# The third batch's loads moved to the software DMA queue, behind the output weights

## The chip, the core and the metric

One core of a Trainium2 chip runs the whole kernel. The metric is device time in microseconds (us) per execution: the median of three runs. The matmul engine is PE (TensorE), the vector engine DVE (VectorE), the activation engine ACT (ScalarE), the general engine POOL (GpSimd), and SP (SyncE) only issues transfers. A core has 16 DMA engines. Transfers issued by SP go on queue q1 (its descriptors are made in hardware), those issued by POOL on queue q0 (made in software on POOL); only POOL's transfers change the type on the way, from float32 in DRAM to bf16 on chip.

## The reference

Inputs q, k and v are float32 of shape (8 batches, 8 heads, 576 rows, 64). Attention with pooled keys and values feeds a gated layer:

```
k_p, v_p = mean of k, v over groups of 8 rows        # 72 rows
attn     = softmax(q @ k_p.T / 8);  x = attn @ v_p   # x: 4608 x 512
h        = x @ w_in                                  # 512 x 2048
out      = (h * cos(h)) @ w_out                      # 2048 x 512
```

## The kernel before

The schedule is written out by hand: each engine runs its instructions in the order of the program. Attention for batch b gives 576 rows of `xT`. The gated layer works in nine tiles (`t` = 0 to 8) of 512 rows: `up` (lines 252 to 263) multiplies by the input weights into three pairs of PSUM banks, ACT takes the cosine into a tile `cos`, DVE multiplies into `g_sb`, and `down_mm` (line 265) multiplies by the output weights. The attention of batch `t + 1` is woven into the `down` matmuls of tile t (lines 333 to 369).

Before the loop stands a start (lines 283 to 324). POOL issues, in this order: k of batch 0 (`k_b`, four transfers), q of batch 0 (`q_main`, `q_rem`, four), v of batch 0 (two), the input weights (four), k, q and v of batch 1 (two each), the output weights (four). SP issues k and v of batch 2 (lines 300 and 301) at the same time, as float32, into the two `kv_st` buffers: a main piece of 64 partitions and a rest of 8 each, 1.18 MB per tensor. Then PE pools k of batch 0 with matmuls (line 142), transposes q (line 168), makes scores, sums and values (lines 199, 208, 222); the values' first step pools v (line 150). The first `up` follows.

From batch 2 on, k and v are pooled on POOL (`pool_kv`, lines 114 to 120, three additions each) out of `kv_st`. At the end of tile t's step the program emits `pool_kv` for batch t + 2. `load_kv` of the batch after waits on SP until `kv_st` is free again; q goes on POOL's queue (`load_q`, line 90) in tile t's step, for batch t + 2. In the step of tile 1, PE transposes the pooled k of batch 2 (line 190), and later uses its v.

A tile that is asked for again waits until its oldest buffer of the same name is free: `kv_st` has two buffers, `q_main` and `q_rem` two each, `cos` three. POOL's transfers count on eight semaphores in turn, so a ninth transfer waits until the first has landed.

Of the kernel before, what the change touches and what calls it, by code (L numbers as in the profile page):

```python
# [9 lines left out]
FP32 = mybir.dt.float32  # L10
# [5 lines left out]
TILE = 512  # L16
# [3 lines left out]
def kernel(  # L20
# [9 lines left out]
    nc = tc.nc  # L30
    B, H, S, D = q.shape
# [16 lines left out]
    wpool = ctx.enter_context(tc.tile_pool(name="wpool", bufs=1))  # L48
    kvb = ctx.enter_context(tc.tile_pool(name="kvb", bufs=4))
    kvst = ctx.enter_context(tc.tile_pool(name="kvst", bufs=2))  # L50
    qst = ctx.enter_context(tc.tile_pool(name="qst", bufs=2))
    asb = ctx.enter_context(tc.tile_pool(name="asb", bufs=2))
    msb = ctx.enter_context(tc.tile_pool(name="msb", bufs=3))
    psum = ctx.enter_context(tc.tile_pool(name="psum", bufs=1, space=bass.MemoryType.PSUM))
# [12 lines left out]
    def by_rows(dst, src):  # L67

        for lo, hi in ((0, 64), (64, Sp)):
            yield dst[lo:hi], src[:, lo:hi]  # L70

    def kv_view(src, b):
        return src[b].rearrange("h (p t) d -> h p (t d)", t=POOL)

    def load_kv(b, which, src):
        st = kvst.tile([Sp, H, POOL, D], FP32, name="kv_st", tag="kv_st")
        for o, i in by_rows(st.rearrange("p h t d -> p h (t d)"), kv_view(src, b)):
            nc.sync.dma_start(out=o, in_=i.rearrange("h p n -> p h n"))
        staged[which, b] = st

    def load_kv_cast(b, which, src, halves=1):
# [8 lines left out]
    def load_q(b, halves=1):  # L90
        qm = qst.tile([128, H, 4, D], BF16, name="q_main", tag="q_main")
        qr = qst.tile([64, H, D], BF16, name="q_rem", tag="q_rem")
        hs = H // halves
        for j in range(halves):
            hh = slice(j * hs, (j + 1) * hs)
            nc.gpsimd.dma_start(out=qm[:, hh].rearrange("p h t d -> p h (t d)"),
                                in_=q[b, hh, 0:512, :].rearrange("h (p t) d -> p h (t d)", t=4))
            nc.gpsimd.dma_start(out=qr[:, hh], in_=q[b, hh, 512:S, :].rearrange("h s d -> s h d"))
        pooled["q", b] = (qm, qr)
# [6 lines left out]
    def load_w_out(cg):  # L106
        nc.gpsimd.dma_start(
            out=w_out_sb[cg],
            in_=moe_w_out[cg * 512:(cg + 1) * 512, :].rearrange("(f p) m -> p f m", p=128))
# [23 lines left out]
    def pool_k_mm(b, bank, pjs):  # L133

        kb = staged["k", b]
        if ("kpT", b) not in att:
            att["kpT", b] = asb.tile([128, KCH, Sp], BF16, name="kpT", tag="kpT")
        ps = bank[:, 0:KCH * Sp].rearrange("p (j n) -> p j n", j=KCH)
        for pj in pjs:
            for t in range(POOL):  # L140
                for hp in range(2):
                    nc.tensor.matmul(ps[hp * 64:hp * 64 + 64, pj, :], lhsT=kb[:, 2 * pj + hp, t, :],  # L142
                                     rhs=identity[:Sp, :Sp], start=(t == 0), stop=(t == POOL - 1))
        sl = slice(pjs[0], pjs[-1] + 1)
        nc.vector.tensor_copy(out=att["kpT", b][:, sl, :], in_=ps[:, sl, :])

    def pool_v_mm(b, bank):
        vb = staged["v", b]
        for t in range(POOL):
            nc.tensor.matmul(bank[:Sp, :], lhsT=identity[:Sp, :Sp], rhs=vb[:, :, t, :],  # L150
                             start=(t == 0), stop=(t == POOL - 1))
        dst = asb.tile([Sp, H, D], BF16, name="vp", tag="vp")
        nc.vector.tensor_copy(out=dst, in_=bank[:Sp, :].rearrange("p (h d) -> p h d", h=H))
        pooled["v", b] = dst

    def q_transpose(b, bank, pjs=range(KCH)):

        if ("qT", b) not in att:
            att["qT", b] = asb.tile([128, KCH, S], BF16, name="qT", tag="qT")
        qT = att["qT", b]  # L160
        qb, _ = pooled["q", b]
        n = len(pjs)
        ps = bank.rearrange("p a n -> p (a n)").bitcast(BF16)[:, 0:n * 512].rearrange(
            "p (j t n) -> p j t n", t=4, j=n)
        for i, pj in enumerate(pjs):
            for t in range(4):
                for hp in range(2):
                    nc.tensor.matmul(ps[hp * 64:hp * 64 + 64, i, t, :], qb[:, 2 * pj + hp, t, :],  # L168
                                     identity, is_transpose=True)
        c0 = col_of(b, 0)  # L170
        nc.vector.tensor_copy(out=qT[:, pjs[0]:pjs[-1] + 1, c0:c0 + 512],  # L171
                              in_=ps.rearrange("p j t n -> p j (t n)"))

    def q_transpose_rem(b, bank, pjs=range(KCH)):
        qT = att["qT", b]
        _, qrb = pooled["q", b]
        n = len(pjs)
        ps = bank.bitcast(BF16)[:, 0:n * 64].rearrange("p (j n) -> p j n", j=n)
        for i, pj in enumerate(pjs):
            nc.tensor.matmul(ps[:, i, :], heads(qrb, pj).rearrange("p h d -> p (h d)"),  # L180
                             identity[:64, :64], is_transpose=True)
        c0 = col_of(b, 4)
        nc.vector.tensor_copy(out=qT[:, pjs[0]:pjs[-1] + 1, c0:c0 + 64], in_=ps)  # L183
# [61 lines left out]
    def exp_tables():  # L245
        nc.scalar.preload_act_table_set("natural_log_exp_and_others")  # L246
# [5 lines left out]
    def up(t, fp):  # L252

        h = banks[fp % 3]
        for j in range(2):
            fc = 2 * fp + j
            for ki in range(KCH):
                nc.tensor.matmul(h[:, j, :], lhsT=w_in_sb[fc // 4][:, ki, (fc % 4) * 128:(fc % 4 + 1) * 128],  # L258
                                 rhs=xT[:, ki, t * TILE:(t + 1) * TILE],
                                 start=(ki == 0), stop=(ki == KCH - 1))  # L260
        cos = msb.tile([128, 2, TILE], FP32, name="cos", tag="cos")
        nc.scalar.activation(out=cos, in_=h, func=ACTF.Sin, bias=half_pi[:, :1])  # L262
        nc.vector.tensor_mul(out=g_sb[:, 2 * fp:2 * fp + 2, :], in0=h, in1=cos)  # L263

    def down_mm(o, ms, fc):
        nc.tensor.matmul(o, lhsT=g_sb[:, fc, ms * 128:(ms + 1) * 128],  # L266
                         rhs=w_out_sb[fc // 4][:, fc % 4, :], start=(fc == 0), stop=(fc == FFCH - 1))
# [29 lines left out]
    load_kv_cast(1, "v", v)  # L297
    for cg in range(4):
        load_w_out(cg)
    load_kv(2, "k", k)  # L300
    load_kv(2, "v", v)
    exp_tables()
    LAG = 4
    for j in range(2):
# [21 lines left out]
    for t in range(NT):  # L326
        b = t + 1
        for fp in range(FFCH // 2):
            up(t, fp)
            if t == 0 and fp == 5:  # L330
                pool_k_mm(1, obanks[0], range(KCH))
        more = b < B
        fill = []
        if t == 0:
            outs = [obanks[0], obanks[1], banks[2][:, 0, :], banks[2][:, 1, :]]
            mms = [(ms, fc) for cg in range(4) for ms in range(4) for fc in range(4 * cg, 4 * cg + 4)]
            exp_tables()
            q_transpose(1, banks[0])
            q_transpose_rem(1, banks[1][:, 0, :])
            pool_v_mm(1, banks[1][:, 1, :])  # L340
            main = att_main(1, [banks[0]], banks[1])
            fill = [(i * 7 // 2, f) for i, f in enumerate(main)]
        else:
            outs = [obanks[ms % 2] for ms in range(4)]
            mms = [(ms, fc) for ms in range(4) for fc in range(FFCH)]
            if more:
                early = [lambda: k_transpose(b, banks[2][:, 0, :]),
                         lambda: q_transpose(b, banks[0]),
                         lambda: q_transpose_rem(b, banks[2][:, 1, :])]
                main = att_main(b, [banks[1], banks[0]], banks[2])  # L350
                fill = [(4 + 4 * i, f) for i, f in enumerate(early)]
                fill += [(16 + (i * 5) // 2, f) for i, f in enumerate(main)]
                exp_tables()
        if more and t > 0 and b + 1 < B:
            load_kv(b + 1, "k", k)
            load_kv(b + 1, "v", v)
        if more and b + 1 < B:
            load_q(b + 1)
        fi = 0
        for n, (ms, fc) in enumerate(mms):  # L360
            while fi < len(fill) and fill[fi][0] <= n:
                fill[fi][1]()
                fi += 1
            down_mm(outs[ms], ms, fc)
            if fc == FFCH - 1:
                down_out(t, ms, outs[ms])
        while fi < len(fill):
            fill[fi][1]()
            fi += 1
        if more:  # L370
            sin_tables()
            if b + 1 < B:
                pool_kv(b + 1, "k", nc.gpsimd)
                pool_kv(b + 1, "v", nc.gpsimd)
# [30 lines left out]
```

## Time and profile before

| what | us |
|---|---|
| median of 3 runs | 374.42 (374.41 to 374.74) |
| profiled execution, its own time | 373.32 |
| span of that execution, first to last instruction | 371.6 |
| PE busy | 332.1 (89% of the span) |
| ACT, DVE, POOL busy | 191.8, 156.4, 124.2 |

Times within the profile count from the first instruction. Clock columns give the share of full speed that was granted to PE: 1.00 is 2.4 GHz, 0.50 is 1.2 GHz. GB/s counts the bytes written, so a transfer that turns float32 into bf16 counts two bytes per element.

### The profile page before, as it was taken

To read this page: it belongs to the slowest core of one execution; us is meant where nothing else is said; L and a number is where in the kernel's file an instruction comes from. 1 tells how busy PE (TensorE), PEld (TensorE's weight loads), DVE (VectorE), ACT (ScalarE), POOL (GpSimd) and SP (SyncE) were. 2 spreads that over 40 slices of the span, in tenths; PEclk is the share of its full clock that TensorE was granted. 3 is DMA by queue.
4 is the path that set the end of the run, shared out by engine and by line. 5 is a ranking of instruction groups with operands and counts; after the bars stand their busy time and mean duration, and the time that the engine had idled before them with its cause. 6 is when DMAs were issued, how large, how long until landed. Compare 5 with 4: busy or idle time off the path is not lost.

```text
span 371.6 us, 4965 instructions
## 1 busy us (share of the span) xinstructions
PE 332.1 (89%) x1992; PEld 137.7 (37%) x1992; DVE 156.4 (42%) x201; ACT 191.8 (52%) x280; POOL 124.2 (33%) x80
## 2 busy tenths in 40 slices
PE   0158697998999899989998999899989998999995
PEld 0133244333442344334423442344334433444442
DVE  0021356114662366236632663275337533742641
ACT  1017464364657565756575657565756575611610
POOL 6143299200099009800980098019600000000000
PEclk9999999699999999999999999999999999999999
DMA  7999999502942694169426941693020001002002
GB/s 144 192 149 198 153 188 129 65 1 86 192 92 59 98 201 77 59 111 185 89 53 114 188 91 41 118 196 85 30 58 0 30 28 58 0 28 86 0 30 83
DMA packets 31990, 35.18 MB, mean 95 GB/s; under 512 B 5856, under 2 KB 20448, under 8 KB 31968
## 3 DMA queue, kind: packets, MB, share of 16 engines
q1 hardware_dynamic: 12448, 23.60, 27.6%
q0 software_dynamic: 19520, 11.28, 26.3%
q8 instruction: 15, 0.25, 0.3%
q14 instruction: 7, 0.06, 0.1%
HBM read 36.70 MB, written 9.44 MB: 124 GB/s over the span
## 4 chain that ended last, share of the span: by engine, by line
PE 86%; DMA 5%; DVE 3%; ACT 3%; POOL 1%; issue 1%; DVEq 0%; POOLq 0%
PE bank L258 34%; PE obank L266 34%; DMA q_main<-in_q_dram 5%; PE bank L199 4%; PE bank L208 4%; PE bank L222 3%; PE bank L168 2%; PE bank L150 2%; PE bank L266 2%; DVE xT L227 2%; ACT inv L214 1%; ACT lnc L212 1%; POOL k_b L87 1%; DVE o_sb L271 1%; DVE qT L171 0%
## 5 line engine op out<-in xcount | busy, mean ns | idle before, releaser
L266 PE MATMUL obank<-w_out_sb,g_sb 128*128 128x512 bf16 x544 | 141.4, 383 | 0.0
L258 PE MATMUL bank<-xT,w_in_sb 128*128 128x512 bf16 x576 | 127.6, 382 | 0.0
L262 ACT ACTIVATE cos<-bank,half_pi 128x1024 f32<-128x1024 f32 x72 | 80.2, 1115 | 75.7 <-PE bank L258 75.7
L263 DVE TENSOR_TENSOR g_sb<-bank,cos 128x1024 bf16<-128x1024 f32 x72 | 88.2, 1225 | 54.0 <-ACT cos L262 54.0
L117 POOL TENSOR_TENSOR kv_st<-kv_st 72x2048 f32<-72x2048 f32 x12 | 54.2, 4519 | 110.5 <-DMA kv_st<-in_k_dram 110.5
L258 PEld LDWEIGHTS <-w_in_sb 128*128 128x128 bf16 x576 | 56.6, 99 | 68.9 <-issue 2.4
L266 PEld LDWEIGHTS <-g_sb 128*128 128x128 bf16 x576 | 45.9, 98 | 60.0 <-issue 15.0
L202 ACT ACTIVATE ex<-bank 72x576 bf16<-72x576 f32 x64 | 41.0, 641 | 49.9 <-PE bank L199 48.5
L227 DVE TENSOR_TENSOR xT<-bank,inv 128x288 bf16<-128x288 f32 x64 | 29.3, 458 | 88.9 <-ACT inv L214 84.7
L212 ACT ACTIVATE lnc<-bank 128x288 f32<-128x288 f32 x56 | 23.0, 411 | 32.2 <-PE bank L222 32.2
L271 DVE COPY o_sb<-obank 128x512 f32<-128x512 f32 x34 | 23.4, 687 | 29.4 <-PE obank L266 29.4
L214 ACT ACTIVATE inv<-lnc 128x288 f32<-128x288 f32 x64 | 28.3, 443 | 2.0
L118 POOL TENSOR_TENSOR kv_st<-kv_st 72x1024 f32<-72x1024 f32 x12 | 28.2, 2349 | 0.9
L208 PE MATMUL bank<-ex,ones 72*64 72x288 bf16 x112 | 17.5, 307 | 6.3 <-DVE xT L227 6.3
L222 PE MATMUL bank<-ex,vp 72*64 72x288 bf16 x128 | 20.1, 303 | 3.1 <-DVE xT L227 3.1
L199 PE MATMUL bank<-qT,kpT 64*72 64x288 bf16 x128 | 21.5, 331 | 0.4 <-DVE qT L183 0.4
L142 PE MATMUL obank<-identity,k_b 72*64 72x72 bf16 x128 | 3.6, 227 | 19.2 <-DMA k_b<-in_k_dram 19.2
L208 PEld LDWEIGHTS <-ones 72*64 72x64 bf16 x128 | 8.5, 109 | 32.7 <-issue 32.7
L199 PEld LDWEIGHTS <-kpT 64*72 64x72 bf16 x128 | 7.4, 110 | 26.9 <-issue 26.9
L168 PE MATMUL bank<-identity,q_main 128*64 128x128 bf16 x256 | 9.7, 232 | 2.9 <-DMA q_main<-in_q_dram 2.1
L171 DVE COPY qT<-bank 128x2048 bf16<-128x2048 bf16 (+1 forms) x9 | 9.9, 1105 | 5.1 <-PE bank L168 5.1
L246 ACT ACT_TABLE_LOAD x8 | 10.3, 1283 | 0.9 <-PEq L389 0.7
(34 smaller groups left out, 113.3 us busy)
## 6 DMA issues: line engine op xcount, KB each, us to landing
out_dram<-o_sb SPq DMA_DIRECT2D x32, 256.0 KB, 2.3
kv_st<-in_k_dram SPq DMA_DIRECT2D x6, 1024.0 KB, 8.2
kv_st<-in_v_dram SPq DMA_DIRECT2D x6, 1024.0 KB
q_main<-in_q_dram POOLq DMA_DIRECT2D x7, 512.0 KB, 6.0
w_in_sb<-in_moe_w_in_dram POOLq DMA_DIRECT2D x4, 512.0 KB, 13.2
w_out_sb<-in_moe_w_out_dram POOLq DMA_DIRECT2D x4, 512.0 KB, 15.5
v_b<-in_v_dram POOLq DMA_DIRECT2D x2, 512.0 KB, 16.5
out_dram<-o_sb SPq DMA_DIRECT2D x8, 128.0 KB, 2.3
```

What stands on the lines that cost most here:

```text
L117: eng.tensor_tensor(out=s[:, :, 0:4, :], in0=s[:, :, 0:4, :], in1=s[:, :, 4:8, :], op=ADD)
L118: eng.tensor_tensor(out=s[:, :, 0:2, :], in0=s[:, :, 0:2, :], in1=s[:, :, 2:4, :], op=ADD)
L199: nc.tensor.matmul(pair[:Sp, hp, :SEG], lhsT=kpT[hp * 64:hp * 64 + 64, pj, :], rhs=qT[hp * 64:hp * 64 + 64, pj, sg * SEG:(sg + 1) * SEG])
L202: nc.scalar.activation(out=ex, in_=pair[:Sp, :, :SEG], func=ACTF.Exp, scale=scale / POOL)
L208: nc.tensor.matmul(cs[hp * 64:hp * 64 + 64, :SEG], lhsT=ones[:Sp, :], rhs=ex[:, hp, :])
L214: nc.scalar.activation(out=inv, in_=lnc, func=ACTF.Exp, scale=-1.0)
L222: nc.tensor.matmul(ao[hp * 64:hp * 64 + 64, :SEG], lhsT=vp[:, 2 * pj + hp, :], rhs=ex[:, hp, :])
L227: nc.vector.tensor_mul(out=xT[:, pj, c0:c0 + SEG], in0=ao[:, :SEG], in1=att.pop(("inv", b, i)))
L258: nc.tensor.matmul(h[:, j, :], lhsT=w_in_sb[fc // 4][:, ki, (fc % 4) * 128:(fc % 4 + 1) * 128], rhs=xT[:, ki, t * TILE:(t + 1) * TILE], st ...
L262: nc.scalar.activation(out=cos, in_=h, func=ACTF.Sin, bias=half_pi[:, :1])
L263: nc.vector.tensor_mul(out=g_sb[:, 2 * fp:2 * fp + 2, :], in0=h, in1=cos)
L266: nc.tensor.matmul(o, lhsT=g_sb[:, fc, ms * 128:(ms + 1) * 128], rhs=w_out_sb[fc // 4][:, fc % 4, :], start=(fc == 0), stop=(fc == FFCH - 1))
```

## The change

The loads of k and v of batch 2 go on POOL's queue in place of SP's, at the end of the start's loads, and q of batch 2 is loaded between them in place of in the step of tile 0. `q_main` and `q_rem` get a third buffer, `cos` has two buffers in place of three. Loads of batches 3 to 7 keep their place.

```
-    qst = ctx.enter_context(tc.tile_pool(name="qst", bufs=2))
+    qst = ctx.enter_context(tc.tile_pool(name="qst", bufs=3))
...
-    def load_kv(b, which, src):
+    def load_kv(b, which, src, queue=nc.sync):
...
-            nc.sync.dma_start(out=o, in_=i.rearrange("h p n -> p h n"))
+            queue.dma_start(out=o, in_=i.rearrange("h p n -> p h n"))
...
-        cos = msb.tile([128, 2, TILE], FP32, name="cos", tag="cos")
+        cos = msb.tile([128, 2, TILE], FP32, name="cos", tag="cos", bufs=2)
...
         load_w_out(cg)
-    load_kv(2, "k", k)
-    load_kv(2, "v", v)
+    load_kv(2, "k", k, nc.gpsimd)
+    load_q(2)
+    load_kv(2, "v", v, nc.gpsimd)
     exp_tables()
...
         if more and t > 0 and b + 1 < B:
             load_kv(b + 1, "k", k)
             load_kv(b + 1, "v", v)
-        if more and b + 1 < B:
             load_q(b + 1)
```

## Rows read from the trace of the kernel before

**Rows 1.** The page: busy time by engine, the chain that ended last.

```profile
PE 332.1 (89%) x1992; PEld 137.7 (37%) x1992; DVE 156.4 (42%) x201; ACT 191.8 (52%) x280; POOL 124.2 (33%) x80
...
PE 86%; DMA 5%; DVE 3%; ACT 3%; POOL 1%; issue 1%; DVEq 0%; POOLq 0%
```

**Rows 2.** The chain that ended last, first 70 us: start us, us, what.

```profile
5.79 19.14 DMA q_main<-in_q_dram
...
24.98 1.08 PE bank L168 x16
...
31.60 3.56 PE bank L150 x8
...
43.88 12.05 PE bank L258 x48
...
68.39 1.40 PE obank L266 x3
```

**Rows 3.** DMA queues from 0 to 7.6, then 7.6 to 25 us.

```profile
q1 hardware_dynamic: 521, 1.06, 67.7%
...
q0 software_dynamic: 2816, 1.62, 104.0%
q1 hardware_dynamic: 679, 1.30, 44.1%
```

**Rows 4.** DMA issues and packets from 65.3 to 66.9 us, one batch's q alone.

```profile
DMA packets 0, 0.00 MB, mean 0 GB/s; under 512 B 0, under 2 KB 0, under 8 KB 0
...
q_main<-in_q_dram POOLq DMA_DIRECT2D x1, 512.0 KB, 6.0
```

**Rows 5.** Stretches: busy time of each engine, granted clock, DMA share, GB/s.

```profile
10.00:17.00 7.00, 1.17 (x32) 1.05 (x32) 0.31 (x1) 0.00 (x0) 1.27 (x2) 1.00 1.16 205
17.00:20.00 3.00, 0.00 (x0) 0.00 (x0) 0.00 (x0) 0.00 (x0) 0.40 (x1) 1.00 1.90 119
25.00:37.00 12.00, 10.59 (x56) 4.49 (x57) 1.97 (x4) 7.79 (x18) 4.68 (x7) 1.00 1.31 194
92.90:107.70 14.80, 14.80 (x92) 6.95 (x92) 9.79 (x9) 10.15 (x9) 4.68 (x2) 1.00 0.89 178
```

**Rows 6.** POOL, one DVE copy, SPq: start us, us, engine, line, [idle before, releaser].

```profile
1.25 2.53 POOL L87 DMA_DIRECT2D k_b<-in_k_dram  x4 [0.80 <-POOLq L389]
...
13.74 0.69 POOL L87 DMA_DIRECT2D v_b<-in_v_dram  x1 [6.54 <-DMA k_b<-in_k_dram]
...
25.22 1.27 POOL L87 DMA_DIRECT2D k_b<-in_k_dram  x2 [1.09 <-DMA q_main<-in_q_dram]
...
26.09 0.69 DVE L171 COPY qT<-bank 128x1024 bf16<-128x1024 bf16 x1 [1.75 <-PE bank L168]
...
48.83 4.55 POOL L117 TENSOR_TENSOR kv_st<-kv_st 72x2048 f32<-72x2048 f32 x1
...
65.34 0.92 POOL L96 DMA_DIRECT2D q_main<-in_q_dram  x1
...
92.70 1.19 SPq L78 DMA_DIRECT2D kv_st<-in_k_dram  x2
```

**Rows 7.** PE in tile 1's down stage: first uses of batch 2.

```profile
106.00 0.29 PE L190 MATMUL bank<-identity,kp 72*128 72x72 bf16 x4
...
112.19 0.29 PE L222 MATMUL bank<-ex,vp 72*64 72x288 bf16 x2
```

**Rows 8.** ACT and DVE at the start of tile 1's up stage.

```profile
96.71 1.11 ACT L262 ACTIVATE cos<-bank,half_pi 128x1024 f32<-128x1024 f32 x1 [0.61 <-PE bank L258]
...
94.40 1.23 DVE L263 TENSOR_TENSOR g_sb<-bank,cos 128x1024 bf16<-128x1024 f32 x1 [2.18 <-ACT cos L262]
```

**Rows 9.** Stretches around tile 0's change from up to down; the clock stands third from last.

```profile
60.70:64.40 3.70, 1.36 (x36) 1.27 (x36) 3.18 (x4) 2.38 (x2) 3.54 (x3) 0.96 0.55 61
64.40:71.00 6.60, 6.56 (x18) 2.11 (x18) 0.69 (x1) 1.29 (x2) 2.54 (x3) 0.50 0.76 90
```

**Rows 10.** The page's DMA issues: KB each, median us from issue to landing.

```profile
w_out_sb<-in_moe_w_out_dram POOLq DMA_DIRECT2D x4, 512.0 KB, 15.5
```

## The prediction

> **What bounds the kernel now.** I read the page first. PE is busy 89% of the span and carries 86% of the chain that ended last; a DMA carries 5% [rows 1]. So nearly all of the time is matmuls that this change doesn't touch, and the one thing it can shorten is that DMA. The chain of waits says where it lies: a single piece, q of batch 0, issued at 5.79 us and waited for during 19.14 us, until PE starts its second half of q transposes at 24.98 [rows 2]. From there to the end the chain holds work of the engines alone, so an earlier 24.98 moves the whole rest forward, as long as no later transfer comes onto the chain.
>
> Why is q so late? The DMA queues by stretch tell it. Up to 7.6 us every packet is SP's queue q1 (1.06 MB), which carries only k and v of batch 2; from 7.6 to 25 us POOL's queue q0 brings 1.62 MB and q1 another 1.30 MB [rows 3]. The stretches then show a pipe that is full: 205 GB/s from 10 to 17 us with both queues, 194 GB/s from 25 to 37 us with q0 alone [rows 5]. So the third batch, first needed by PE at 106 us [rows 7], takes 44% of what is moved while PE waits for the first.
>
> **What goes.** Without q1 the two tensors that PE waits for, k and q of batch 0 (0.59 MB each as bf16), have the pipe to themselves. The unknown is when q0's first packet comes. In the trace it is 7.6 us, 6.3 us after POOL's first issue at 1.25 [rows 3, 6]; a q load into an idle pipe has no packet for 1.6 us after its issue at 65.34 [rows 4, 6]. So either the first use of POOL's queue costs those 4.7 us more whatever q1 does, or q1 kept it back. After 7.6 us both queues move side by side, which speaks against a q1 that shuts q0 out, so I take the first: q0 still starts at 7.6.
>
> Then the sum: k takes 0.59 MB / 194 GB/s = 3.0 us [rows 5]. I add 0.4 us, an estimate: its two 8-row pieces (0.066 MB) can only use part of the engines, and at half of 194 GB/s they take 0.34 us longer. q takes what the lone load takes from its first packet at 66.9 to its landing at 65.34 + 6.0 = 71.3, that is 4.4 us [rows 4, 6]. So q lands at 7.6 + 3.0 + 0.4 + 4.4 = 15.4, against 24.98: **9.6 us earlier**. Bounds: if k and q only go at the 119 GB/s of the slow stretch from 17 to 20 us [rows 5], their 1.18 MB take 9.9 us, q lands at 17.5 and the gain is 7.5. If q0 starts 1.6 us after its issue, at 2.9, q lands at 10.7 and the gain is 14.3. Of these ends I stay near the middle because the start at 7.6 is seen, and the lone q load is the nearest row for the rate.
>
> The Trainium skill, "DMA: Bandwidth & Descriptors", section Anatomy of one DMA, gives about 2.0 us plus bytes / 436 GB/s for a transfer on this path. As an estimate, 1.18 MB would then take 2.7 us plus a 1 us tail after 7.6, and the gain would be 13.7. The rows nowhere show such a rate for bf16 over a whole stretch (194 GB/s), so the sum goes by the rows.
>
> **What is late next.** Everything below is moved 9.6 us forward on the compute side, and queued by the rates above on the DMA side.
> - v of batch 0: 15.4 + 3.4 = 18.8; its pooling stands at 31.60 [rows 2], then at 22.0. Covered by 3.2 us, the smallest margin.
> - Input weights: 2.10 MB / 194 GB/s = 10.8 us, so 29.6; the first up matmul moves from 43.88 [rows 2] to 34.3.
> - k, q, v of batch 1: 33.0, 37.4 and 40.8; the first is wanted in the up stage and v just before the first down matmul, which moves from 68.39 to 58.8 [rows 2].
> - Output weights: 51.6, against 58.8, and only their first quarter is wanted then.
>
> **What is added and moved.** POOL gets four more issues (two per tensor) of about 0.63 us (2.53 us for four [rows 6]), 2.5 us, in a stretch where it mostly waits for transfers; SP loses four, which nobody waited for. Behind the output weights come k of batch 2 (1.18 MB at 178 GB/s, the rate of such a load alone [rows 5]: 6.6 us, so 58.2), q (62.6, by the lone load's 4.4) and v (69.2). POOL pools each tensor in half of 48.83 to 65.34, 8.3 us [rows 6]: k at 66.5, v at 77.5. Before, POOL did this from 48.83 to 65.34; so it ends 12 us later. Who waits? PE's transpose of the pooled k moves from 106.0 to 96.4 and the use of v from 112.19 to 102.6 [rows 7]: covers of 30 and 25 us. SP's loads of batch 3 need both buffers; they move from 92.70 [rows 6] to 83.1, cover 5.6 us, and if that is gone SP's output transfers queue behind them, but nothing is due there until tile 1's down stage. Batch 3's q is issued by POOL after the pooling, at 77.5 in place of 65.34, and is wanted two stages later. All this costs nothing on the chain.
>
> The third q buffer takes away a wait for a buffer that was long free, no time. The second-of-three `cos` buffer matters if ACT must wait for DVE: the cosine at 96.71 would need the product of the cosine two before it, and that ran from 94.40 to 95.63 [rows 8], so 1.1 us of cover remains in each of the 72 rounds: nothing.
>
> One more term has no fixed size. PE's clock is 0.50 (1.2 GHz) from 64.4 to 71.0, after a stretch in which PE was busy 1.36 of 3.70 us [rows 9]. That low stretch costs about half of its 6.6 us, 3.3. The same work is there after the change, shifted; I take 0, with about 1.5 us either way.
>
> **The sum.** The profiled execution took 373.3: 373.3 - 9.6 = 363.7. The three runs stand 1.1 above it at the median, so **364.8**.
>
> **The rivals.**
> - *The late start was contention too* (0.30): q0 starts at 2.9 and the gain is 14.3: 374.4 - 14.3 = 360.1. For it: POOL's issue instructions were over by 3.78 us and its later transfers start after 1.6. Against it: q0's packets come in at once and then share the pipe.
> - *The start is helped less* (0.08): q0 is slow by itself at the 119 GB/s of 17 to 20 us, when q1 had nearly run out; gain 7.5 or a little less: 367 to 368.
> - *The third batch comes too late, slower than before* (0.03). Place: POOL's queue behind the output weights. If its transfers went one after another, each only after the one before had landed, at the 15.5 us of an output weight [rows 10], the six new ones would take 93 us after 51.6; v's rest would land at 144.6, be pooled at 152.9, and PE would wait 50 us for it at 102.6: 364.8 + 50 = 415. PE begins to wait when v lands after 102.6 - 8.3 = 94.3, and the time passes the old one when it lands after 103.9, 35 us later than in my sum. Against it: POOL runs eight transfers ahead (v of batch 0, the ninth, is the first to wait for k's landing [rows 6]). Another way to the same lateness is POOL being held up by DVE while it issues; two issues at 25.22 took 1.27 us, 0.63 each as at the start, although DVE copied from 26.09 [rows 6], so no hold shows. The Trainium skill, "DMA: Bandwidth & Descriptors", section SWDGE vs HWDGE vs iDMA, speaks for that way: it gives plain transfers to SP or ACT, since POOL writes its descriptors into on-chip memory from which DVE can lock it out.
> - *No effect* (0.02): if k and q of batch 0 were held by something else than q1 until 25 us, the time stays 374.4.
>
> **The numbers.** My forecast has 0.57, the rivals 0.30, 0.08, 0.03 and 0.02. This measurement can tell about 0.2% (0.75 us) from no change. Faster: 0.57 + 0.30 + 0.08 = 0.95; the same 0.02; slower 0.03. My own case spans 363 to 367 with the clock term; the contention rival pulls the low end to 359.3, the slower start the high end to 368. Some 1 in 10 is left out.
>
> **What would show it.** In the new profile q1 has no packet before the first output, near 78 us. q0's first packet tells my case (7.6 us) from the contention rival (2.9). The chain's wait for q should end at 15.4, the first up matmul stand at 34.3 and the first down matmul at 58.8, and after that each stage should last as before. POOL's first addition should stand near 58. I am wrong if PE shows a new wait for v, for weights or for the pooled k, if ACT waits for DVE at the cosine, or if the low-clock stretch changes by several us.

## The result and the profile after

The changed kernel takes **360.76 us** (360.34 to 360.95) against 374.42 (374.00 to 374.74): ratio 0.9634, interval 0.9618 to 0.9651, faster by 13.7 us. The profiled execution took 360.34, 13.0 less than that of before; beside the first four runs below, the kernel before has a median of 373.80 (372.40 to 374.75, 19 executions), also 13.0 above 360.76. So the last 0.7 of the 13.7 is within the spread of the kernel before.

The chain that ended last, of the changed kernel (start us, us, what), answers to [rows 2]:

```profile
5.79 5.91 DMA q_main<-in_q_dram
...
11.75 1.08 PE bank L168 x16
...
30.99 11.72 PE bank L258 x47
...
55.18 0.54 PE obank L266
...
354.37 0.69 DVE o_sb L271
```

The wait for q is 5.91 us in place of 19.14: q has landed at 11.70, not at 24.94. The second half of the q transposes stands 13.2 us earlier, the first up stage 12.9, the first down matmul 13.2, and the last piece of the chain, DVE's copy, moves from 367.58 to 354.37, 13.2. So the whole gain is made before the second half of the q transposes and carried to the end. (Where a count is a matmul short, as x47, a record is missing.)

The DMA queues of the changed kernel, from 0 to 2.9 us and then from 0 to 7.6, where [rows 3] have q1 alone:

```profile
q0 software_dynamic: 16, 0.02, 3.8%
...
q0 software_dynamic: 874, 0.68, 68.8%
```

POOL's queue brings its first packets between 2.7 and 2.8 us, 1.5 us after its first issue, and has moved 0.68 MB by 7.6, where in the kernel before it was only starting. That is the contention rival, not my case.

The later deadlines, in the changed kernel: POOL's first addition and SP's next loads by their queues, then PE's first uses of batch 2, as in [rows 6, 7]:

```profile
52.21 4.50 POOL L117 TENSOR_TENSOR kv_st<-kv_st 72x2048 f32<-72x2048 f32 x1 [11.65 <-DMA kv_st<-in_k_dram]
...
68.74 0.91 POOL L96 DMA_DIRECT2D q_main<-in_q_dram  x1
...
79.49 1.38 SPq L78 DMA_DIRECT2D kv_st<-in_k_dram  x2
...
92.79 0.29 PE L190 MATMUL bank<-identity,kp 72*128 72x72 bf16 x4
...
98.98 0.29 PE L222 MATMUL bank<-ex,vp 72*64 72x288 bf16 x2
```

POOL waits 11.65 us for the third batch, but it is through with both tensors at 68.74, while SP comes for the buffers at 79.49 and PE for the pooled k at 92.79, each 13.2 us earlier than before. The late place of these loads costs nothing.

### The profile page after: what moved, and what is told of

It is laid out like the page before. It is cut to its first block, busy times and chain, and to the rows that moved or that the text cites. A ratio compares the mean times of both kernels' runs of the same rounds, so it can differ in the third digit from the quotient of the medians.

```text
span 358.6 us, 4924 instructions
## 1 busy us (share of the span) xinstructions
PE 328.5 (92%) x1958; PEld 137.6 (38%) x1992; DVE 156.4 (44%) x201; ACT 191.8 (53%) x280; POOL 126.9 (35%) x84
## 4 chain that ended last, share of the span: by engine, by line
PE 88%; DVE 3%; ACT 3%; issue 2%; DMA 2%; POOL 1%; DVEq 0%; POOLq 0%
PE bank L258 35%; PE obank L266 34%; PE bank L199 4%; PE bank L208 4%; PE bank L222 3%; PE bank L168 2%; PE bank L150 2%; PE bank L266 2%; DVE xT L227 2%; DMA q_main<-in_q_dram 2%; ACT inv L214 1%; ACT lnc L212 1%; POOL k_b L87 1%; DVE o_sb L271 1%; DVE qT L171 1%
## 5 line engine op out<-in xcount | busy, mean ns | idle before, releaser
L266 PE MATMUL obank<-w_out_sb,g_sb 128*128 128x512 bf16 x522 | 138.0, 383 | 2.6 <-issue 2.1
L262 ACT ACTIVATE cos<-bank,half_pi 128x1024 f32<-128x1024 f32 x72 | 80.2, 1114 | 75.7 <-PE bank L258 75.1
## 6 DMA issues: line engine op xcount, KB each, us to landing
w_out_sb<-in_moe_w_out_dram POOLq DMA_DIRECT2D x4, 512.0 KB, 13.7
```

## The experiments

**The move alone.** The kernel before with only its four loads moved:

```
...
-    load_kv(2, "k", k)
-    load_kv(2, "v", v)
+    load_kv(2, "k", k, nc.gpsimd)
+    load_kv(2, "v", v, nc.gpsimd)
...
```

> The kernel before with one part of the change: the four loads of batch 2's k and v go on POOL's queue behind the output weights; q of batch 2 stays in tile 0's step, q keeps two buffers, cos three. My theory (the move is all of the gain): 360.8 us, within 0.7 of the changed kernel, first q0 packet near 2.8, q of batch 0 landed at 11.7. The rival (the third q buffer and the early q of batch 2 have a part): 362 or more, with POOL's additions or a q transpose late.

Measured: 360.57 us (359.77 to 361.12), ratio 0.9643 (0.9618 to 0.9668). The chain has:

```profile
5.82 5.68 DMA q_main<-in_q_dram
...
11.54 1.08 PE bank L168 x16
```

As the theory has it. The third q buffer, the early q of batch 2 and the shorter `cos` together are worth nothing that shows.

**On SP's queue, but later.** The loads stay on q1 and wait for a DVE memset of a corner of `kv_st`, behind the last q copy:

```
+    def load_kv_after(b, which, src, eng):
+        st = kvst.tile([Sp, H, POOL, D], FP32, name="kv_st", tag="kv_st")
+        eng.memset(st[:, 0, 0, :], 0.0)
...
-    load_kv(2, "k", k)
-    load_kv(2, "v", v)
...
         q_transpose_rem(0, banks[1][:, 0, :], pjs)
+    load_kv_after(2, "k", k, nc.vector)
+    load_kv_after(2, "v", v, nc.vector)
```

> The kernel before, with batch 2's k and v still on SP's queue, but behind a DVE memset of a corner of each kv_st that stands after the last q copy of batch 0 (about 13.8 us), so q1 starts near 15 and shares the pipe with the input weights. Theory 'only the first 12 us count': q lands at 11.7 as in the changed kernel; weights and batch 1 land up to 12 us later than there but still inside their covers, 360.8 us. Rival 'the place behind the output weights counts too': q1 takes two thirds of the pipe while it lasts, an up or down matmul waits for its weights, 363 to 368.

Measured: 360.59 us (360.01 to 361.70), ratio 0.9647 (0.9615 to 0.9679). The queues from 18 to 36 us, then the chain:

```profile
q0 software_dynamic: 1668, 1.64, 59.4%
q1 hardware_dynamic: 1189, 2.35, 59.3%
```

```profile
5.79 6.63 DMA q_main<-in_q_dram
...
31.38 11.97 PE bank L265 x48
...
55.81 1.40 PE obank L273 x3
```

All 2.35 MB share the pipe with q0's loads, the input weights first, in 18 us, and no matmul waits for it: the first up and down matmuls stand within 0.7 us of the changed kernel's. (q lands at 12.42 here, at 11.50 in the run before this one and at 11.70 in the changed kernel, so a single landing is good to about 0.5 us.) So neither the software queue nor the place behind the output weights earns the time. What counts is that these bytes keep out of the pipe until q of batch 0 is in.

**On SP's queue, just behind batch 0's k.** The same memset, on POOL, behind the four issues of k:

```
     load_kv_cast(0, "k", k, 2)
+    load_kv_after(2, "k", k, nc.gpsimd)
+    load_kv_after(2, "v", v, nc.gpsimd)
```

> The kernel before, with batch 2's k and v on SP's queue behind a POOL memset that stands after POOL's four issues of batch 0's k (about 3.9 us), so q1's first packet comes near 5.5, some 2.7 us behind q0's. Theory A (a queue that has come first keeps the other out for one whole transfer, then they share): q0 starts at 2.8, k's first half lands near 5.5, then q0 stands still for about 5 us or shares at a third, q lands at 16 to 20, 365 to 370 us. Theory B (q0 is late only because its first packet is late; sharing costs little): q lands near 13, 362.

Measured: 374.35 us (373.13 to 374.98), ratio 1.0014 (0.9997 to 1.0031): nothing gained, worse than either theory. The queues from 2 to 6 us, from 7.5 to 9, and from 9 to 20:

```profile
q0 software_dynamic: 470, 0.42, 82.2%
...
q1 hardware_dynamic: 154, 0.32, 86.8%
q0 software_dynamic: 16, 0.00, 2.0%
...
q1 hardware_dynamic: 903, 1.78, 87.4%
q0 software_dynamic: 1035, 0.40, 35.7%
```

q0 starts at once and has 0.42 MB by 6 us. Then q1 comes and q0 all but stops for 1.5 us; after that it gets 0.40 MB in 11 us against q1's 1.78. PE's second q transposes stand at 25.25. So an early first packet is worth nothing by itself: theory B falls, and of theory A the standstill is seen (q0's issues of q were over by 7.4, and from 7.5 to 9 it has 16 packets with next to no bytes), but the sharing behind it costs more than I gave it.

**The same bytes at once, in smaller transfers.** The main pieces cut into four transfers of two heads each:

```
...
+        for j in range(0, H, 2):
+            nc.sync.dma_start(out=to[0:64, j:j + 2], in_=fr[0:64, j:j + 2])
...
```

> The kernel before, with the main piece of batch 2's k and of its v each cut into four transfers of two heads (256 KB), at once on SP's queue as before. Theory A (q0 has to wait until q1's first transfer is through): q0's first packet comes at 3 to 4 us in place of 7.6 and q lands about 4 us earlier, 370 us. Theory C (what holds q0 back is all that q1 has queued, whatever the size of a transfer): q0's first packet stays at 7.6 or later, 374.4.

Measured: 373.54 us (372.61 to 374.38), ratio 0.9990 (0.9974 to 1.0006). The queues from 3 to 4 us, then from 13 to 17, and the chain:

```profile
q0 software_dynamic: 131, 0.13, 83.5%
q1 hardware_dynamic: 78, 0.13, 33.5%
...
q1 hardware_dynamic: 374, 0.69, 84.2%
q0 software_dynamic: 374, 0.19, 37.2%
```

```profile
24.54 1.08 PE bank L176 x16
```

Half right. q0 now moves 0.13 MB between 3 and 4 us, where with one large transfer it had nothing until 7.6: it is q1's first transfer as one piece that keeps q0 out. But q is still late (PE goes on at 24.54). The second pair of lines shows why: each queue gets 374 packets. By its size a packet of the profile is one descriptor, which here is one unbroken piece of a tile: eight rows of 64 float32 on q1, 2048 bytes, and four rows of 64 bf16 for q on q0, 512 bytes. So the two take turns by descriptor, and q1 takes 78% of the bytes. The kernel before, from 11 to 15 us, and the run with the loads behind q, from 20 to 29 us, where q0's descriptors write 1024 bytes, show the same turns:

```profile
q1 hardware_dynamic: 273, 0.56, 75.4%
q0 software_dynamic: 271, 0.25, 37.8%
...
q1 hardware_dynamic: 667, 1.32, 70.0%
q0 software_dynamic: 667, 0.66, 46.3%
```

**The same turns with smaller descriptors.** The cut goes across the eight rows of a group, with the same number and size of transfers:

```
...
+        for j in range(0, POOL, 2):
+            nc.sync.dma_start(out=to[0:64, :, j * D:(j + 2) * D], in_=fr[0:64, :, j * D:(j + 2) * D])
...
```

> The kernel before, with the main piece of batch 2's k and of its v each cut into four transfers, as in the run that cut them by heads (q landed at 24.5 there, 373.5 us), but cut across the eight rows of a group, so that one descriptor writes 512 bytes in place of 2048; number, size and time of the transfers are the same. Theory D (the two queues take turns descriptor by descriptor, so q1 gets the larger part because its descriptors are larger): q0 now gets half to two thirds of the pipe, q of batch 0 lands at 14 to 17, 363.5 to 367 us. Rival E (they take turns by transfer, or share by bytes, or q1 goes first whatever the sizes): q lands near 24.5, 373.5 us.

Measured: 368.04 us (367.56 to 368.53), ratio 0.9838 (0.9811 to 0.9866). The queues from 15 to 18 us, then the chain:

```profile
q0 software_dynamic: 711, 0.27, 73.2%
q1 hardware_dynamic: 713, 0.35, 62.0%
```

```profile
5.80 13.14 DMA q_main<-in_q_dram
...
18.98 1.08 PE bank L176 x16
```

Again equal turns (711 and 713), and with descriptors of 512 bytes q1 no longer outweighs q0 by nearly four to one. q lands 5.6 us earlier than in the run before this, 5.5 us of time. Rival E falls. q and the time lie 2 and 1 us beyond what theory D gave: q's rest goes in descriptors of 64 bf16, 128 bytes, which I had not counted, and early on q1 was still ahead, by 0.26 MB to 0.08 from 2 to 4 us and by 695 packets to 104 from 5 to 7. So the equal turns hold from the time when transfers of both queues are under way, not from the first packet on.

**Half of the bytes.** The changed kernel with only k of batch 2 back on SP's queue:

```
-    load_kv(2, "k", k, nc.gpsimd)
+    load_kv(2, "k", k)
```

> The changed kernel with k of batch 2 back on SP's queue at once, v staying behind the output weights. Theory F (whatever q1 has ahead goes almost wholly before q, so the delay is its bytes): half of 13.2 us, q lands at 18.3, 367.4 us. Rival G (q1's first transfer shuts q0 out until 7.6, after that q0 is alone): q lands near 16.5, 365.5. Rival H (any load on q1 at the start costs the whole): 374.

Measured: 364.50 us (364.28 to 364.72), ratio 0.9743 (0.9718 to 0.9769). The queues from 0 to 7 us, then from 8 to 17, and the chain:

```profile
q1 hardware_dynamic: 473, 0.97, 65.2%
...
q0 software_dynamic: 2714, 1.59, 136.5%
q1 hardware_dynamic: 37, 0.06, 8.0%
```

```profile
5.79 10.43 DMA q_main<-in_q_dram
...
16.26 1.08 PE bank L168 x16
```

That is rival G: q0 is shut out while k goes, is then nearly alone, and q lands at 16.22. Half of the bytes delay q not by half of 13.2 but by 4.5 us (the time is 3.7 us above the changed kernel's). This run parts the loss in two: **4.5 us** (16.22 - 11.70) for k alone, as much as q0's first packet is later (7.2 against 2.7), and **8.7 us** (24.94 - 16.22) for v behind it, which shares by turns. The parts don't come off singly: the run cut by heads all but took the shut-out away, and q came only 0.4 us earlier, since both tensors still shared by turns.

**Can the start go faster still?** Two runs on top of the changed kernel. First, POOL's constants behind its issues of q:

```
+    load_q(0, 2)
     identity = consts.tile([128, 128], BF16, name="identity")
...
-    load_q(0, 2)
```

> The changed kernel with POOL's identity, ones and half_pi (0.65 us of POOL from 3.75 us) moved behind its issues of batch 0's q, so that these stand 0.65 us earlier. If POOL's issue paces the start now (in the changed kernel the pipe moves only 99 KB from 5 to 6 us): q lands 0.4 to 0.65 us earlier, 360.2 us. If the pipe paces it: no difference, 360.7.

Then also one transfer in place of two for each rest of batch 0:

```
+            if j == 0:
+                nc.gpsimd.dma_start(out=qr, in_=q[b, :, 512:S, :].rearrange("h s d -> s h d"))
```

> As the run before this one, and batch 0's k rest (8 rows) and q rest go in one transfer each in place of two halves, which takes two issues (1.2 us) of POOL out of the start. If POOL's issue paces the start: q lands 1 to 1.5 us earlier than in the changed kernel, 359.5 us. If the pipe does: 360.7.

Measured: 360.87 us (360.48 to 361.57) and 360.73 (359.62 to 362.70), beside 360.76: no difference that can be told. PE's second q transposes do come earlier, at 11.17 and 11.00 in place of 11.75, so POOL's issues seem to have a part in when q lands. PE's rows of the first up stage, in the changed kernel, in the first of these runs and in the second (start us, us):

```profile
30.99 11.72 PE L258 MATMUL bank<-xT,w_in_sb 128*128 128x512 bf16 x47 [0.33 <-issue]
...
43.80 3.63 PE L258 MATMUL bank<-xT,w_in_sb 128*128 128x512 bf16 x15
```

```profile
30.00 12.98 PE L258 MATMUL bank<-xT,w_in_sb 128*128 128x512 bf16 x48
...
44.08 3.63 PE L258 MATMUL bank<-xT,w_in_sb 128*128 128x512 bf16 x16
```

```profile
29.82 12.14 PE L264 MATMUL bank<-xT,w_in_sb 128*128 128x512 bf16 x48
...
43.05 3.63 PE L264 MATMUL bank<-xT,w_in_sb 128*128 128x512 bf16 x16
```

The first starts the stage about 1 us earlier than the changed kernel and has lost it again by the stage's last 16 matmuls (44.08 against 43.80). The second still has 0.75 us of its 1.2 there, and its profiled execution took 359.62 against 360.34, but its five executions lie 3.1 us apart, so this can't be told from no change. The last section comes back to this. No version here can be told from the changed kernel as faster.

## Why the prediction was right in the range and wrong in its case

- **The place and the kind were right.** I had put the whole gain on the wait for q of batch 0 and on the bytes that q1 moves during it. The chain shows that, and the run with the move alone and the run with the loads later on SP's own queue show it twice more, by other edits.
- **The step that failed** is "so I take the first: q0 still starts at 7.6". It starts between 2.7 and 2.8. My argument was that both queues move side by side after 7.6, so q1 can't have shut q0 out before. Both happen: the run cut by heads shows that the shut-out belongs to q1's first large transfer, the run behind k shows it again when q1 comes second. What I gave a chance of 0.30 was the case; its 360.1 stands 0.7 below the measured 360.76. That the whole range held the time is owed to this rival, which pulled its low end to 359.3: my own case, 363 to 367, did not hold it.
- **The way from q0's start to q's landing was a little too short in my sum.** I had 7.8 us; the changed kernel takes 11.70 - 2.7 = 9.0 and the run with k on SP 16.22 - 7.2 = 9.0. With the start at 7.6 I had 15.4, and 9.0 would have made it 16.6. This is most of why the rival's gain of 14.3 came out as 13.2 in the profile. In the changed kernel a part of it seems to be POOL's issues, which I had left out: from 5 to 6 us the pipe moves only 0.10 MB, and with q's issues earlier q landed 0.6 us earlier.
- **A share was counted late.** The 44% that I gave to q1 holds from 7.6 us on; from the start to 25 us it moved 2.36 of 3.98 MB, 59%.
- **The covers held.** No wait for v, for weights or for the pooled k came onto the chain, as said. `cos` with two buffers costs nothing: ACT's waits at the cosine are for PE, 75.1 us in 71 waits and one of 0.6 without a named releaser, against 75.7 in 72 before. POOL's pooling started at 52.21, not 58, mostly because q had landed 3.7 us earlier than in my sum (11.70 against 15.4), and POOL had ended 10.7 us before SP asked for the buffers.
- **The slow clock** stayed as it was. The stretches of the changed kernel that answer to [rows 9], in their changed place:

```profile
47.50:51.20 3.70, 1.36 (x36) 1.27 (x36) 3.17 (x4) 2.37 (x2) 0.00 (x0) 0.96 1.65 149
51.20:57.80 6.60, 6.36 (x17) 2.15 (x18) 0.69 (x1) 1.29 (x2) 5.51 (x2) 0.51 1.19 202
```

  The granted clock of the second is 0.51 (1.2 GHz for nearly all of it), after a stretch in which PE was busy 1.36 of 3.70 us as before, so the term I set to 0 was 0.
- **The figure of the Trainium skill.** The Trainium skill, "DMA: Bandwidth & Descriptors", section Anatomy of one DMA, had led to an estimate of 13.7, close to the 13.2 and 13.7 that came out, but for another reason: it kept the start at 7.6 and a pipe of 436 GB/s. The start moved, and the pipe went at 191 GB/s from 10 to 17 us. The same page of the Trainium skill, section Queues, rings and completion order, says that an engine goes round the queues that have work, a packet of several descriptors at a time (there a packet is more than a packet of the profile). The equal counts, 374 and 374, agree with turns that don't look at bytes; no run here shows how many descriptors make one turn.

## What to carry to other kernels

A transfer that isn't needed soon is not free because its queue is another one: at the start it takes the pipe from what everybody waits for. See in each queue's bytes up to the landing of the first operand what else was moved, and hold that back with a dependency or a later place; which of the two makes no difference as long as it lands in time. Where two queues share, as here, look at the size of their descriptors: with equal turns the one with the larger descriptors gets the larger part. And a queue's first large transfer can keep the other queue out until it is through.

## What I had not expected of the hardware

Starting q0 early does not help it against q1. With a lead of over 3 us (no packet of q1 until 6 us), or with q1 cut in pieces, q of batch 0 landed at the same time as before (25.2 and 24.5 us), since q1 still took 82% of the bytes from 9 to 20 us in the one run and 78% from 13 to 17 in the other.

Nor does a queue's first large transfer always keep the other out. In the run with the loads behind q, q1's first transfer goes beside q0 from the start, 94 packets to 98 from 19 to 20 us, and here q1 is the one that waited: its first packet came between 18.5 and 18.6, 4.1 us after SP's issue at 14.49. What decides which queue stands still, and for how long, no run here shows.

The 0.6 to 0.75 us that the last two runs gained on q did not reach their medians. The first up stage begins slowly in every run, and the moment at which it becomes fast did not move with its start. Two stretches of the run with the constants behind q, then two of the changed kernel; the first bracket counts the matmuls that run in the stretch, also in part:

```profile
32.00:34.00 2.00, 2.00 (x6) 0.76 (x5) 0.00 (x0) 0.30 (x1) 0.55 (x1) 1.00 1.25 203
...
35.00:37.00 2.00, 2.00 (x11) 0.88 (x10) 1.06 (x1) 0.89 (x1) 1.50 (x3) 1.00 1.25 208
```

```profile
31.00:34.00 3.00, 3.00 (x8) 1.13 (x8) 0.22 (x1) 0.00 (x0) 1.30 (x2) 1.00 1.26 204
34.00:36.00 2.00, 2.00 (x11) 0.90 (x10) 0.68 (x1) 1.27 (x2) 0.88 (x1) 1.00 1.24 205
```

The run that starts the stage earlier, at 30.00, still counts 6 matmuls in 2 us up to 34 and gets to 11 from 35 on; the changed kernel, which starts at 30.99, has 11 from 34 on.

The column of the granted clock shows 1.00 throughout, but here it is no reading: the trace's records of this clock begin only at 33.84 us in the changed kernel, at 34.99 and 33.10 in the last two runs, and at 47.05 in the kernel before, and what is not recorded counts as 1.00. The matmuls tell what the clock was. Pooled v takes PE the same eight matmuls in batch 0, where the column has 1.00, and in batch 1, where it has 0.50 (the chain of the changed kernel):

```profile
18.36 3.56 PE bank L150 x8
...
51.22 3.57 PE bank L150 x8
```

So PE ran at the lower of its two levels, 1.2 GHz, in the attention of batch 0 too. The up stage's matmuls start 0.43 us apart until the records begin and 0.22 apart from then on, so its slow beginning is the lower level, and the jump is the rise to 2.4 GHz. PE is busy without a gap from the stage's start to the rise, which comes 2.9 us after the start in the changed kernel, 5.0 in the run with the constants behind q and 3.3 in the one with fewer issues. The 1 us that a run gains before the stage is lost when the rise comes late, as in the first of the two; what sets the moment of the rise no run here shows.
